# Linear attention plus GELU feed-forward on one core: another order of the input loads ahead of the first matmuls

## Chip, cores and metric

The kernel runs on one core of a Trainium2 chip. The metric is device time in microseconds (us) for one execution; lower is better. Before the change three runs gave a median of 211.41 us (211.33 to 211.56).

## What is computed

One normalised input feeds two branches, and both are added to the input (B = 1, S = 2048 tokens, D = 640, F = 1536, 32 heads of 20 columns; bf16 in and out):

```python
x = A_x
xn = _layernorm(x, axis=-1)
return x + _A_ref(xn, A_wqkv, A_wo) + _B_ref(xn, B_w1, B_b1, B_w2, B_b2)
# _A_ref: q, k, v = xn @ wqkv; phi(t) = where(t > 0, t + 1, exp(t)) + 1e-6
#         o = (phi(q) @ (phi(k)^T v)) / (phi(q) . sum(phi(k)) + 1e-6), per head; o @ wo
# _B_ref: gelu(xn @ w1 + b1) @ w2 + b2
```

## The kernel before

The 2048 tokens are 16 tiles of 128 (t = 0 to 15). `x_in` (named `xPK` in the profile) holds x with the token on the partition, `xn_tm` the normalised x in the same layout, and `xnT` its transpose (feature on the partition), which the matmuls read. The work is written as one list per engine by a small planner class: each instruction goes to the end of its engine's list, in the order of the Python text, and waits for the semaphores of what it reads and overwrites. Nothing is reordered later, so the order of the text is the order on each engine and on SP's DMA queue.

The front, which the change touches, goes as follows.

- **Loads.** SP issues x tile by tile and the weight W1 in four column quarters (`dma_w1`, 480 KB each); x0 is split in two column halves, one from SP and one from ACT. `dma_x(t, n)` loads n tiles from tile t on (160 KB a tile), all through the helper at L242. The order on SP before the loop is: x0's first half, x1, W1 quarters one and two, x2, quarter three, x3, quarter four, x4-5, x6-7. The read of x8-11 is issued behind tile 3's transpose, and that of x12-15 behind tile 8's.
- **Normalise.** For each tile: two statistics instructions on DVE (`ln_half`, L327, one per column half), an aggregate on DVE (`ln_aggr`, L335), a reciprocal root on GpSimd (L341, L343), and a normalise on DVE (`ln_norm`, L355).
- **Transpose.** Tiles 0 to 2 are transposed on PE (`transp2` and `transp`, L313 and L363) into PSUM and copied out: tiles 0 and 1 in two parts, feature blocks 0 to 2 and 3 to 4, one on DVE and one on ACT (`copy2`, L321 and L322), tile 2 by one DVE copy (L371). Tiles 3 to 15 are transposed by DMA (`xnT_dma`, L245), issued on SP, the queue that the x loads use too.
- **First matmuls.** `h_unit(t0, n, jb)` (L382) makes one 128-row block jb of the hidden layer for n tiles: five matmuls, then a GELU on ACT (L386). Block jb needs W1's quarter jb // 3. The order of units is written out by hand:

```python
plan = h_list(0, 1, 0, 3) + ["T1"] + h_list(0, 1, 3, 6) + h_list(1, 1, 0, 6) + h_list(0, 1, 6, 9)
plan += ["T2"] + h_list(1, 1, 6, 9) + h_list(2, 1, 0, JT)
plan += h_list(0, 1, 9, JT) + h_list(1, 1, 9, JT) + h_list(3, 1, 0, JT)
for t, n in ((4, 2), (6, 2), (8, 4), (12, 4)):
    plan += h_list(t, n, 0, JT)
```

At "T1" and "T2" the PE transposes of tiles 1 and 2 are put in, and with them the DVE work of the next tiles. At "T2", after the DVE work of tile 4, `ln_rest()` writes out the normalising and the DMA transposes of all further tiles in one go.

Behind the front, PE computes phi(k), the matrix that joins xn and phi(k), phi(q), the products with Wv and Wo, and at last the output, 17 matmul groups a tile. The change touches no line of these.

Of the kernel before, what the change touches and what calls it, by code (L numbers as in the profile page):

```python
# [6 lines left out]
ACT = mybir.ActivationFunctionType  # L7
P = 128
# [104 lines left out]
def bass_parallel_sum__linear_attn_block__dense_activation_gelu__prompt_kernel(  # L113
# [4 lines left out]
    NT = S // P  # L118
# [3 lines left out]
    DT = D // P  # L122
# [3 lines left out]
    HW = D // 2  # L126
# [3 lines left out]
    Pl = Planner(nc)  # L130
    R_ = Pl.res
# [5 lines left out]
    with contextlib.ExitStack() as es:  # L137
# [3 lines left out]
        x_in = xPK  # L141
# [3 lines left out]
        xnT = xnTf[:].rearrange("p (k s) -> p k s", k=DT)  # L145
# [37 lines left out]
        B_ = [R_("bank%d" % i) for i in range(8)]  # L183
        ring = [0]

        def take(n):
            b = ring[0]
            if n == 2 and b % 2:
                b += 1
            b %= 8  # L190
            ring[0] = (b + n) % 8
            return b

        def bank(b, lo=0, hi=512):
            return ps[:, b * 512 + lo: b * 512 + hi]
# [4 lines left out]
        def halves(ap):  # L200
            return ap.rearrange("p (a n) -> p a n", a=2)

        r_x = [[R_("x%d_%d" % (t, i)) for i in range(2 if t == 0 else 1)] for t in range(NT)]
        r_xr = [R_("xr%d" % c) for c in range(NC)]
        r_xb = [R_("xb%d" % t) for t in range(NT)]
        r_xn = [[R_("xn%d_%d" % (t, i)) for i in range(2 if t == 0 else 1)] for t in range(NT)]
        r_xnT = [[R_("xnT%d_%d" % (t, i)) for i in range(2 if t < 2 else 1)] for t in range(NT)]
# [7 lines left out]
        r_stats = [R_("stats%d" % i) for i in range(4)]  # L215
# [14 lines left out]
        xv = A_x.rearrange("b s d -> (b s) d")  # L230
# [6 lines left out]
        v = "vector"  # L237
        s_ = "scalar"
        pe = "tensor"

        def dma(eng, dst, src, writes, reads=()):
            Pl.ins(eng, lambda e: e.dma_start(dst, src), reads=reads, writes=writes, dma=True)  # L242
# [4 lines left out]
        def dma_x(t, n):  # L247
            dma("sync", x_in[:, t:t + n, :], xv[t * P:(t + n) * P, :].rearrange("(t p) d -> p t d", p=P),
                sum(r_x[t:t + n], []))

        def dma_w1(i):
            lo, hi = W1P[i]
            dma("sync", W1[:, :, lo:hi], w1v[:, :, lo:hi], [r_W1[i]])

        for i, q in enumerate(("sync", s_)):
            dma(q, x_in[:, 0, i * HW:(i + 1) * HW], xv[0:P, i * HW:(i + 1) * HW], [r_x[0][i]])
        dma_x(1, 1)
        dma_w1(0)
        dma_w1(1)
        dma_x(2, 1)  # L260
        dma_w1(2)
        dma_x(3, 1)
        dma_w1(3)
        dma_x(4, 2)
        dma_x(6, 2)

        Pl.ins(v, lambda e: e.memset(warm[:].bitcast(FP32), 0.0), writes=[r_warm])
        Pl.ins(g, lambda e: e.memset(onesm[:], 1.0), writes=[r_ones])
# [5 lines left out]
               reads=[r_ident], writes=[r_ident])  # L274
# [35 lines left out]
        def transp2(t, b0, b1):  # L310
            for lo, hi, b in ((0, 3, b0), (3, DT, b1)):
                pT = bank(b).bitcast(BF16)
                Pl.ins(pe, [(lambda e, k=k, pT=pT, lo=lo: e.transpose(  # L313
                    pT[:, (k - lo) * P:(k - lo + 1) * P], xn_tm[:, t, k * P:(k + 1) * P], ident[:]))
                    for k in range(lo, hi)], reads=[r_xn[t][0 if lo == 0 else -1], r_ident], writes=[B_[b]])

        def copy2(t, b0, b1):
            tok = slice(t * P, (t + 1) * P)
            pA = bank(b0).bitcast(BF16)[:, 0:XA].rearrange("p (k q) -> p k q", q=P)
            pB = bank(b1).bitcast(BF16)[:, 0:D - XA].rearrange("p (k q) -> p k q", q=P)  # L320
            Pl.ins(v, lambda e: e.tensor_copy(xnT[:, 0:3, tok], pA), reads=[B_[b0]], writes=[r_xnT[t][0]])  # L321
            Pl.ins(s_, lambda e: e.activation(xnT[:, 3:DT, tok], pB, ACT.Copy), reads=[B_[b1]],  # L322
                   writes=[r_xnT[t][1]])

        def ln_half(t, h):
            s = t % 4
            Pl.ins(v, lambda e: e.bn_stats(stats[:, s, 6 * h:6 * h + 6], x_in[:, t, h * HW:(h + 1) * HW]),  # L327
                   reads=[r_x[t][min(h, len(r_x[t]) - 1)]], writes=[r_stats[s]])

        def ln_aggr(t):  # L330
            s = t % 4
            if t < 2:
                Pl.ins(v, lambda e: e.tensor_single_scalar(stats[:, s, 2:3], stats[:, s, 2:3], D * EPS, ALU.add),
                       reads=[r_stats[s]], writes=[r_stats[s]])
            Pl.ins(v, lambda e: e.bn_aggr(aggr[:, s, :], stats[:, s, :]),  # L335
                   reads=[r_stats[s]], writes=[r_aggr[s]])
            if t < 2:
                var, r_var = aggr[:, s, 1:2], r_aggr[s]
            else:
                var, r_var = veps[:, s:s + 1], r_veps[s]  # L340
                Pl.ins(g, lambda e: e.tensor_single_scalar(var, aggr[:, s, 1:2], EPS, ALU.add),  # L341
                       reads=[r_aggr[s]], writes=[r_var])
            Pl.ins(g, lambda e: e.tensor_tensor(out=rstd[:, t:t + 1], in0=var, in1=mhalf[:], op=ALU.pow),  # L343
                   reads=[r_var, r_small], writes=[r_rstd[t]])

        def ln_stats(t):
            ln_half(t, 0)
            ln_half(t, 1)
            ln_aggr(t)

        def ln_norm(t):
            s = t % 4
            for i, r in enumerate(r_xn[t]):
                lo, hi = (0, D) if len(r_xn[t]) == 1 else ((0, XA), (XA, D))[i]
                Pl.ins(v, lambda e, lo=lo, hi=hi: e.tensor_scalar(  # L355
                    xn_tm[:, t, lo:hi], x_in[:, t, lo:hi], aggr[:, s, 0:1], rstd[:, t:t + 1],
                    ALU.subtract, ALU.mult),
                    reads=r_x[t] + [r_aggr[s], r_rstd[t]], writes=[r])

        def transp(t):  # L360
            b = take(1)
            pT = bank(b).bitcast(BF16)[:, 0:D]
            Pl.ins(pe, [(lambda e, k=k: e.transpose(pT[:, k * P:(k + 1) * P],  # L363
                                                    xn_tm[:, t, k * P:(k + 1) * P], ident[:]))
                        for k in range(DT)],
                   reads=r_xn[t] + [r_ident], writes=[B_[b]])
            return b

        def xnT_copy(t, b):
            pT = bank(b).bitcast(BF16)[:, 0:D]  # L370
            Pl.ins(v, lambda e: e.tensor_copy(xnT[:, :, t * P:(t + 1) * P],  # L371
                                              pT.rearrange("p (k q) -> p k q", k=DT)),
                   reads=[B_[b]], writes=r_xnT[t])

        def xnT_dma(t):
            dma_t("sync", xnT[:, :, t * P:(t + 1) * P], xn_tm[:, t, :], r_xnT[t], reads=r_xn[t])

        def h_unit(t0, n, jb):
            b = take(1)
            w = n * P  # L380
            tok = slice(t0 * P, t0 * P + w)
            Pl.ins(pe, [(lambda e, k=k: e.matmul(  # L382
                bank(b, 0, w), W1[:, k, jb * P:(jb + 1) * P], xnT[:, k, tok],
                start=(k == 0), stop=(k == DT - 1))) for k in range(DT)],
                reads=[r_W1[FW[jb]]] + sum(r_xnT[t0:t0 + n], []), writes=[B_[b]])
            Pl.ins(s_, lambda e: e.activation(  # L386
                HG[:, jb, tok], bank(b, 0, w), ACT.Gelu_apprx_tanh, bias=b1c[:, jb:jb + 1]),
                reads=[B_[b], r_b1c], writes=[r_HG[t][jb] for t in range(t0, t0 + n)])

        Pl.ins(s_, lambda e: e.activation(b1c[:, 0:1], warm[:, 0:1], ACT.Gelu_apprx_tanh),  # L390
               reads=[r_warm], writes=[r_b1c])
# [24 lines left out]
        def ln_rest():  # L416
            for t in range(4, NT):
                if t + 1 < NT:
                    ln_half(t + 1, 0)
                    ln_half(t + 1, 1)  # L420
                ln_norm(t)
                if t + 1 < NT:
                    ln_aggr(t + 1)
                xnT_dma(t)
                if t == 8:
                    dma_x(12, 4)

        for u in plan:
            if u == "T1":
                b = take(2)  # L430
                transp2(1, b, b + 1)
                copy2(1, b, b + 1)
                ln_stats(2)
                ln_half(3, 0)
                ln_norm(2)
                ln_half(3, 1)
                ln_aggr(3)
            elif u == "T2":
                b = transp(2)
                xnT_copy(2, b)  # L440
                ln_half(4, 0)
                ln_norm(3)
                xnT_dma(3)
                dma_x(8, 4)
                ln_half(4, 1)
                ln_aggr(4)
                ln_rest()
            else:
                h_unit(*u)
# [203 lines left out]
        t = NT - 1  # L653
        xb(t)
        tok = slice(t * P, (t + 1) * P)
        for i, (lo, hi) in enumerate([(0, 320), (320, 512), (512, 640)]):
# [3 lines left out]
            s = t % 2  # L660
            Pl.ins(v, lambda e, lo=lo, hi=hi, b=b: e.tensor_tensor(
                out=out_sb[:, s, lo:hi], in0=bank(b, 0, hi - lo), in1=x_res[:, t, lo:hi], op=ALU.add),
                reads=[B_[b], r_xb[t]], writes=[r_o] + ([r_out[s]] if i == 0 else []))
# [40 lines left out]
```

## Time and profile before

| what | value |
|---|---|
| median of three runs | 211.41 us (211.33 to 211.56) |
| the profiled execution | 211.35 us, of which the profiled span is 209.6 us |
| TensorE (PE) busy | 203.2 us, 97% of the span |
| VectorE (DVE) busy | 108.9 us, 52% |
| ScalarE (ACT) busy | 73.8 us, 35% |
| GpSimd (POOL) busy | 20.0 us, 10% |
| granted TensorE clock | 1.0 |
| hidden-layer matmuls (L382) | 477 records, 52.9 us |
| moved by DMA | 18.16 MB, mean 87 GB/s over the span |

All times in the views are us from the span's start. A row of a timeline gives the start, the time taken, the engine (SPq is SP's list of DMA issues), the line of the kernel, the operation with what it writes and reads, and in square brackets how long the engine stood idle before it and what ended that. For a DMA the row's time is that of the issue; when its data has landed stands in the DMA rows as "us to landing". Busy shares are averages: where a change touches one stage, the waits of that stage count.

### The profile page before, as it was taken

The page shows a single profiled execution, that of the slowest core. Times are in us where ns is not written, and L with a number is a line of the kernel's source. Part 1 is how long each engine was busy: PE and PEld are TensorE (multiplying, and loading weights), DVE is VectorE, ACT ScalarE, POOL GpSimd, SP SyncE. Part 2 cuts the span into 40 slices and gives each one's busy share as a digit, 9 for nine tenths or more (in the row PEclk, how much of TensorE's full clock was granted, in tenths as well). Part 3 has the DMA queues.
Part 4 walks back from the last instruction along what each step waited for, and adds up shares of the span by engine and source line. Part 5 has one row for each costly group of instructions (what it writes and reads, how often), then busy time and mean ns, then how long its engine had stood idle before and what let it go on. Part 6 is the DMA issues. An engine that isn't in the chain of part 4 may idle for free.

```text
span 209.6 us, 3964 instructions
## 1 busy us (share of the span) xinstructions
PE 203.2 (97%) x1616; PEld 140.6 (67%) x1622; DVE 108.9 (52%) x213; ACT 73.8 (35%) x146; POOL 20.0 (10%) x57
## 2 busy tenths in 40 slices
PE   7899699999999999999999999999999999999995
PEld 2799588444447777777757556677777777777775
DVE  4688847000005888999148889633753422523322
ACT  2699588566667445211143556200000000000000
POOL 2134425810011000000000000000000000000000
PEclk9999999999999999999999999999999999999999
DMA  5959965799500000000000000952210110010002
GB/s 147 343 165 190 110 183 111 186 355 341 200 0 0 0 3 0 3 0 0 0 3 0 0 2 14 353 179 57 69 66 31 48 51 31 31 34 31 31 31 66
DMA packets 23515, 18.16 MB, mean 87 GB/s; under 512 B 9928, under 2 KB 23496, under 8 KB 23496
## 3 DMA queue, kind: packets, MB, share of 16 engines
q1 hardware_dynamic: 23136, 17.68, 30.0%
q8 instruction: 13, 0.21, 0.4%
q10 hardware_dynamic: 360, 0.22, 0.4%
q14 instruction: 6, 0.05, 0.1%
HBM read 12.62 MB, written 2.62 MB: 73 GB/s over the span
## 4 chain that ended last, share of the span: by engine, by line
PE 88%; DMA 6%; SPq 2%; DVE 1%; issue 1%; POOL 0%
PE ps L620 35%; PE ps L382 19%; PE ps L494 10%; PE ps L482 10%; PE ps L531 10%; DMA xPK<-in_A_x_dram 3%; DMA xnT<-xn_tm 3%; SPq L242 2%; PE ps L556 1%; PE ps L540 1%; PE ps L571 1%; DVE xn_tm L355 0%; POOL rstd L343 0%; DVE stats L327 0%; PE ps L514 0%
## 5 line engine op out<-in xcount | busy, mean ns | idle before, releaser
L382 PE MATMUL ps<-xnT,W 128*128 128x128 bf16 (+2 forms) x477 | 52.9, 272 | 2.2 <-DMA xnT<-xn_tm 1.9
L620 PE MATMUL ps<-W,HG 128*128 128x320 bf16 (+2 forms) x396 | 54.7, 295 | 0.0
L382 PEld LDWEIGHTS ps<-xnT,W 128*128 128x128 bf16 x480 | 36.8, 98 | 17.9 <-DMA xnT<-xn_tm 2.0
L620 PEld LDWEIGHTS ps<-W,HG 128*128 128x128 bf16 x396 | 38.0, 98 | 14.7 <-issue 0.4
L386 ACT ACTIVATE HG<-ps,b1c 128x128 bf16<-128x128 f32 (+2 forms) x96 | 41.5, 474 | 14.2 <-PE ps L382 12.6
L631 DVE TENSOR_TENSOR W<-ps,xnT 128x640 bf16<-128x640 f32 x15 | 12.4, 824 | 37.1 <-PE ps L620 36.8
L470 ACT ACTIVATE ek<-ps 128x512 bf16<-128x512 f32 (+1 forms) x36 | 23.2, 644 | 20.7 <-PE ps L531 11.0
L471 DVE TENSOR_SCALAR ek<-ek 128x512 bf16<-128x512 bf16 (+1 forms) x36 | 10.9, 303 | 36.8 <-ACT ek L470 35.6
L620 PE MATMUL ps<-Msb,PQ 128*128 128x320 bf16 (+2 forms) x165 | 24.2, 295 | 0.0
L482 PE MATMUL ps<-Wqkv,xnT 128*128 128x320 bf16 x160 | 21.9, 299 | 0.0
L494 PE MATMUL ps<-xPK,xn_tm 128*128 128x320 bf16 x160 | 21.9, 299 | 0.0
L531 PE MATMUL ps<-xnT,Wqkv 128*128 128x512 bf16 x97 | 21.4, 379 | 0.2
L620 PEld LDWEIGHTS ps<-Msb,PQ 128*128 128x128 bf16 x165 | 15.9, 98 | 5.9
L482 PEld LDWEIGHTS ps<-Wqkv,xnT 128*128 128x128 bf16 x160 | 15.6, 98 | 6.3
L494 PEld LDWEIGHTS ps<-xPK,xn_tm 128*128 128x128 bf16 x160 | 15.6, 98 | 6.1
L327 DVE BATCH_NORM_STATS2 stats<-xPK 128x6 f32<-128x320 bf16 x32 | 15.3, 477 | 7.4 <-DMA xPK<-in_A_x_dram 6.7
L531 PEld LDWEIGHTS ps<-xnT,Wqkv 128*128 128x128 bf16 x100 | 11.7, 117 | 9.5
L473 DVE SCALAR_TENSOR_TENSOR PQ<-ps,ek 128x512 bf16<-128x512 f32 x20 | 13.8, 692 | 2.1
L473 DVE SCALAR_TENSOR_TENSOR xPK<-ps,ek 128x640 bf16<-128x640 f32 x16 | 13.2, 825 | 1.7
L506 DVE TENSOR_TENSOR Msb<-Msb,xPK 128x640 f32<-128x640 f32 x14 | 11.6, 826 | 0.5
L498 ACT ACTIVATE W<-ps 128x640 bf16<-128x640 f32 x5 | 3.5, 703 | 18.2 <-PE ps L494 18.2
L355 DVE TENSOR_SCALAR xn_tm<-xPK,aggr,rstd 128x640 bf16<-128x640 bf16 (+2 forms) x17 | 7.2, 431 | 2.5 <-POOL rstd L343 1.5
(57 smaller groups left out, 76.8 us busy)
## 6 DMA issues: line engine op xcount, KB each, us to landing
xnT<-in_A_x_dram SPq DMA_DIRECT2D x4, 640.0 KB, 6.4
Wqkv<-in_A_wqkv_dram SPq DMA_DIRECT2D x3, 800.0 KB, 6.6
out_dram<-W SPq DMA_DIRECT2D x15, 160.0 KB, 1.8
W<-in_B_w_dram SPq DMA_DIRECT2D x4, 480.0 KB, 6.3
W<-in_B_w_dram SPq DMA_DIRECT2D x1, 1920.0 KB, 15.7
xPK<-in_A_x_dram SPq DMA_DIRECT2D x2, 640.0 KB, 4.8
Wo<-in_A_wo_dram SPq DMA_DIRECT2D x1, 800.0 KB, 10.7
xPK<-in_A_x_dram SPq DMA_DIRECT2D x2, 320.0 KB, 7.0
```

What stands on the lines that cost most here:

```text
L327: Pl.ins(v, lambda e: e.bn_stats(stats[:, s, 6 * h:6 * h + 6], x_in[:, t, h * HW:(h + 1) * HW]), reads=[r_x[t][min(h, len(r_x[t]) - 1)]], ...
L382: Pl.ins(pe, [(lambda e, k=k: e.matmul(bank(b, 0, w), W1[:, k, jb * P:(jb + 1) * P], xnT[:, k, tok], start=(k == 0), stop=(k == DT - 1))) ...
L386: Pl.ins(s_, lambda e: e.activation(HG[:, jb, tok], bank(b, 0, w), ACT.Gelu_apprx_tanh, bias=b1c[:, jb:jb + 1]), reads=[B_[b], r_b1c], wri ...
L470: Pl.ins(s_, lambda e: e.activation(e2, src, ACT.Exp), reads=br, writes=[r_ek[s]])
L471: Pl.ins(v, lambda e: e.tensor_scalar(et, et, 1.0, 1e-6, ALU.min, ALU.add), reads=[r_ek[s]], writes=[r_ek[s]])
L473: Pl.ins(v, lambda e: e.scalar_tensor_tensor(out=d2, in0=src, scalar=0.0, in1=e2, op0=ALU.max, op1=ALU.add), reads=br + [r_ek[s]], writes= ...
L482: fns.append(lambda e, k=k, h=h, b=b, t=t: e.matmul(bank(b + h, 0, HW), xnT[:, k, t * P:(t + 1) * P], Wqkv[:, k, D + h * HW:D + (h + 1) * ...
L494: Pl.ins(pe, [(lambda e, t=t, h=h, b=b, f=f, i=i: e.matmul(bank(b + h, 0, HW), xn_tm[:, t, f * P:(f + 1) * P], PK[:, t, h * HW:(h + 1) * H ...
L506: Pl.ins(v, lambda e, t=t: e.tensor_tensor(out=zsum, in0=zsum, in1=PK[:, t, :], op=ALU.add), reads=[r_PK[t], r_zsum], writes=[r_zsum])
L531: Pl.ins(pe, [(lambda e, k=k, j=j, b=b: e.matmul(bank(b), Wqkv[:, k, j:D:DT], xnT[:, k, cc], start=(k == 0), stop=(k == DT - 1))) for k in ...
L620: Pl.ins(pe, [(lambda e, i=i, x=x, bb=bb: e.matmul(bank(bb, 0, x[1] - x[0]), seq[i][0], seq[i][1][:, x[0]:x[1]], start=(i == 0), stop=(i = ...
L631: Pl.ins(v, lambda e: e.tensor_tensor(out=halves(out_sb[:, s, :]), in0=pair(b), in1=halves(x_res[:, t, :]), op=ALU.add), reads=B_[b:b + 2] ...
```

## The change

It puts the loads at the front in another order on SP's queue: x3 in front of W1's third quarter, x4-5 in front of the fourth, x8-11 at the end of the first batch (in front of tile 3's DMA transpose) and x12-15 behind tile 7's transpose instead of tile 8's. x0 is loaded whole by SP. In the copies of tiles 0 and 1 out of PSUM, ACT takes the three-block part and DVE the two-block part. On DVE, tile 3's second statistics move in front of tile 2's normalise, and tile 4's first statistics in front of tile 2's copy.

```diff
-        r_x = [[R_("x%d_%d" % (t, i)) for i in range(2 if t == 0 else 1)] for t in range(NT)]
+        r_x = [[R_("x%d" % t)] for t in range(NT)]
...
-        for i, q in enumerate(("sync", s_)):
-            dma(q, x_in[:, 0, i * HW:(i + 1) * HW], xv[0:P, i * HW:(i + 1) * HW], [r_x[0][i]])
+        dma_x(0, 1)
         dma_x(1, 1)
         dma_w1(0)
         dma_w1(1)
         dma_x(2, 1)
+        dma_x(3, 1)
         dma_w1(2)
-        dma_x(3, 1)
+        dma_x(4, 2)
         dma_w1(3)
-        dma_x(4, 2)
         dma_x(6, 2)
+        dma_x(8, 4)
...
-            Pl.ins(v, lambda e: e.tensor_copy(xnT[:, 0:3, tok], pA), reads=[B_[b0]], writes=[r_xnT[t][0]])
-            Pl.ins(s_, lambda e: e.activation(xnT[:, 3:DT, tok], pB, ACT.Copy), reads=[B_[b1]],
-                   writes=[r_xnT[t][1]])
+            Pl.ins(s_, lambda e: e.activation(xnT[:, 0:3, tok], pA, ACT.Copy), reads=[B_[b0]], writes=[r_xnT[t][0]])
+            Pl.ins(v, lambda e: e.tensor_copy(xnT[:, 3:DT, tok], pB), reads=[B_[b1]], writes=[r_xnT[t][1]])
...
-                   reads=[r_x[t][min(h, len(r_x[t]) - 1)]], writes=[r_stats[s]])
+                   reads=r_x[t], writes=[r_stats[s]])
...
-                if t == 8:
+                if t == 7:
                     dma_x(12, 4)
...
                 copy2(1, b, b + 1)
                 ln_stats(2)
                 ln_half(3, 0)
+                ln_half(3, 1)
                 ln_norm(2)
-                ln_half(3, 1)
                 ln_aggr(3)
+                ln_half(4, 0)
             elif u == "T2":
                 b = transp(2)
                 xnT_copy(2, b)
-                ln_half(4, 0)
                 ln_norm(3)
                 xnT_dma(3)
-                dma_x(8, 4)
                 ln_half(4, 1)
                 ln_aggr(4)
                 ln_rest()
```

## The prediction

> **What bounds the kernel now.** I read the page first (busy shares and slices), then the chain of waits, then the timelines of PE, SP and DVE over the first 25 us, then the DMA rows of narrow windows. The page says TensorE:
>
> ```profile
> PE 203.2 (97%) x1616; PEld 140.6 (67%) x1622; DVE 108.9 (52%) x213; ACT 73.8 (35%) x146; POOL 20.0 (10%) x57
> PE   7899699999999999999999999999999999999995
> PEclk9999999999999999999999999999999999999999
> ```
>
> PE is full in every slice but the first six, at full clock. So the change, which touches only the front, can win only what PE idles there. The PE timeline has one large hole:
>
> ```profile
> 6.95 1.00 PE L382 MATMUL ps<-xnT,W 128*128 128x128 bf16 x15
> ...
> 11.52 0.44 PE L363 MATMUL ps<-ident,xn_tm 128*128 128x128 bf16 x5
> 11.80 9.38 PE L382 MATMUL ps<-xnT,W 128*128 128x128 bf16 x165
> 23.04 39.16 PE L382 MATMUL ps<-xnT,W 128*128 128x256 bf16 x237 [1.86 <-DMA xnT<-xn_tm]
> ```
>
> The 165 matmuls from 11.80 start 0.0558 us apart, so the next could have started at 11.80 + 9.21 = 21.01; it started at 23.04. The hole is 2.03 us (1.86 by modelled ends). Behind 23.04 PE runs without a hole of note, so a shift there passes to the end one for one. The chain names what the hole waits for:
>
> ```profile
> 15.85 6.48 DMA xnT<-xn_tm
> 22.33 0.70 issue
> 23.04 13.26 PE ps L382 x120
> ```
>
> The first 256-token unit needs tiles 4 and 5. Tile 4's DMA transpose, issued at 15.85, lands at 22.33; the "issue" after it is really tile 5's, issued 17.41, which took 5.5 and landed at 22.94. SP's timeline shows what stood in front of them:
>
> ```profile
> 13.76 1.31 SPq L245 DMA_TRANSPOSE xnT<-xn_tm  x1
> 15.12 0.57 SPq L242 DMA_DIRECT2D xPK<-in_A_x_dram  x1
> 15.85 8.03 SPq L245 DMA_TRANSPOSE xnT<-xn_tm  x5
> ```
>
> Tile 3's transpose, with an empty queue, took 2.67 us to land (16.43). Then comes the 640 KB read of x8-11 (lands 19.67), and the next two transposes take 6.5 and 5.5. The DMA rows of 19 to 21 us add a second cause:
>
> ```profile
> GB/s 333 297 287 302 277 282 287 246 210 169 256 251 272 584 256 425 236 266 251 251 266 154 154 97 41 15 10 0 0 0 0 0 0 0 5 10 5 10 5 10
> q14 instruction: 1, 0.01, 5.8%
> q8 instruction: 1, 0.02, 3.3%
> ```
>
> Two instruction fetches start at 19.68 and 19.76 (1.07 and 1.85 us in the trace). From 20.4 the queue trickles at 5 to 10 GB/s: [...] the rest hold their packets open (1.3 us instead of 0.018). Last, DVE:
>
> ```profile
> 10.54 0.49 DVE L327 BATCH_NORM_STATS2 stats<-xPK 128x6 f32<-128x320 bf16 x1 [0.68 <-DMA xPK<-in_A_x_dram]
> ...
> 12.89 0.49 DVE L327 BATCH_NORM_STATS2 stats<-xPK 128x6 f32<-128x320 bf16 x1 [0.40 <-DMA xPK<-in_A_x_dram]
> ```
>
> It waits for x3 (lands 10.52) and x4-5 (12.87), both queued behind W1 quarters; that is why tile 3's normalise runs only at 13.30.
>
> **The change part by part.**
>
> *Landings.* In steady flow (340 GB/s from 5 to 12 us) each transfer lands a fixed step after the one in front: a single x tile 0.47, a W1 quarter 1.48, an x pair 0.80 to 0.86. Before: x2 8.57, W1 quarter three 10.05, x3 10.52, quarter four 12.01, x4-5 12.87, x6-7 13.67. Reordered: x2 8.57, x3 9.04, quarter three 10.52, x4-5 11.38, quarter four 12.87, x6-7 13.67, x8-11 13.67 + 2 x 0.80 = 15.27. Bytes and DMA count on SP stay the same.
>
> *x0 whole.* ACT loses one issue (0.41 us, ACT idle then: nothing). DVE's first statistics started at 3.06 on the first half; the second half landed at 3.22 and its statistics started at 3.66. The row nearest to a whole 160 KB tile is x1: 3.18 us, so x0 at 3.98; statistics at 4.00 and 4.53, 0.87 late. The Trainium skill, "DMA: Bandwidth & Descriptors", section "Anatomy of one DMA", fits 2.0 us plus bytes at 436 GB/s: 2.38 us for a tile, so 3.18, and statistics at 3.20 and 3.73, 0.07 late. The same fit gives 2.19 for a half, where the trace has 2.24 and 2.41; x1 is late by a single packet of 0.96 us. I lean to the rule: +0.1, ends 0 and 0.87. Nothing covers it: statistics, reciprocal root, normalise, transposes and copies follow in a row into the matmul at 6.95 (W1's first quarter lands at 6.63 and hides 0.3 at most of a gain).
>
> *Copy halves swapped.* The three-block half goes to ACT: 0.383 for 256 columns and 0.75 ns per column more, an estimate from the 0.37 of its 128-column rows and the 0.703 of 640, gives 0.48; DVE's two-block copy takes 0.29 by its 0.36 and 0.49 rows. For tile 0, ACT starts 0.11 earlier, because the three-block bank is ready first: 6.31 + 0.48 = 6.79 against 6.81. Nothing. For tile 1 it ends 0.1 later (8.75) with 0.25 us to spare before tile 1's first unit at about 9.0.
>
> *Tile 2 and W1 quarter three.* Both statistics of x3 now fit ahead of tile 2's normalise (9.8 to 10.8; reciprocal root ready at 10.83): normalise at 10.86 instead of 10.96. Nothing won, since PE reaches those transposes only at 11.52. Quarter three is first used three units of 0.279 before them, at 10.68, and lands at 10.52: slack 0.63 shrinks to 0.16, or 0.26 with x0's shift. Cost 0 to 0.4.
>
> *Tile 4's first statistics ahead of tile 2's copy.* This is an added wait: DVE holds at x4-5 with tile 2's copy, hence PE's first tile-2 unit (12.64), behind it. Tile 3's aggregate ends at 11.45, x4-5 lands at 11.38, statistics 11.47 to 11.96, copy at 12.00 as now. Tie. Each tenth that x4-5 lands after 11.5 costs a tenth. I book 0.1, ends 0 and 0.6.
>
> *Tile 3.* Reciprocal root ready at 12.4, normalise behind the copy at 12.55 to 13.0 (13.30 before), transpose issued at 13.0 instead of 13.76, but now behind x8-11 on the one queue. Two rows show a transpose behind a 640 KB read: tile 9's landed 0.58 after it, tile 4's 2.66 after it, in the fetches. So 15.85 to 17.93 here; another fetch falls at 12.34, so I take 17.0. PE needs it at 17.66 plus the shift. Cost 0, ends 0 and 0.3.
>
> *Tiles 4 and 5.* The DVE cadence is 1.56 us per tile. Transposes at 15.1 and 16.65 (15.85 and 17.41 before); with no read in front each takes its lone 2.67: 17.8 and 19.3, ahead of the fetch at 19.68 and of the need at 21.2. The hole closes: -2.03. x12-15 goes out behind tile 7's transpose at about 21; tiles 8 to 11 then land by 30, needed at about 34. Hidden.
>
> Sum: -2.03 + 0.1 + 0.1 = -1.83 us. The profiled execution took 211.35 (span 209.6 and 1.75 around it), 0.06 below the median: 209.5 from it, 209.6 from the median 211.41.
>
> **The rivals.**
>
> *x0 late as x1 was* (chance 0.10). For it: x1's own row. Against: both halves were in by 3.22. Cost 0.87 instead of 0.1: 210.35.
>
> *A new wait in the front* (0.10): quarter three, x4-5 in front of tile 2's copy, or tile 3's transpose at its late end. For it: slacks of 0.16, 0.1 and 0.7. Against: each is late by tenths. 0.5 to 1.2 lost: 210.1 to 210.9.
>
> *x8-11 held back on SP, tile 3 behind it* (0.18). The place is the wait of tile 3's first unit at 17.66. SP's issues already stall when much is outstanding: x3's took 1.44 us and the next pairs 1.06 and 0.92, against 0.43 to 0.53. If x8-11 cannot be issued until about 12.9, it lands 4.5 later (its own row) at 17.4, and the transpose 2.66 behind at 20.1: a stall of 2.4 in place of the 2.03, and with x0's 0.1 a time of 211.9. It decides at a landing of 19.6 (no change); past 20.0 it is slower. Against: x6-7's issue ended at 7.78, so at that pace x8-11 is out by 10.
>
> *The change doesn't do what it says*: that the hole is the fetches' alone and stays. Then tile 5 must still be in flight at 19.68; my 19.3 leaves 0.4 us. If hit, it lands at 21.3 to 22.0 and 0.2 to 0.9 of the hole stays: inside the range.
>
> **How the numbers follow.** 0.2% is 0.42 us, about what this kernel's measurement tells from no change. The clean case (0.62) gives 209.1 to 210.1, likeliest 209.6. With the first two rivals, 0.82 lies at 209.1 to 210.9: faster 0.82, and that is the range. The held read (0.18) splits into 0.05 within 0.42 us of 211.41 and 0.13 slower.
>
> **What would show it.** Right: no hole at the start of the 256-token units, which begin near 21.2; x3's statistics without a wait; x4-5 at about 11.4; tile 3's transpose landed by 17.7; tiles 4 and 5 in 2.7 us each. Wrong: the first statistics after 3.5, a hole at 10.7, 12.6 or 17.7, an x8-11 issue later than 11, or the hole merely moved to tile 3.

## The result and the profile after

The changed kernel takes 209.42 us (median of four runs, 209.23 to 209.78) against 211.45 before in the same measurement: ratio 0.9906, 95% interval 0.9889 to 0.9923. That is 2.03 us less; the forecast was 209.6 with faster as the likeliest outcome. The page after, busy shares and slices:

```profile
PE 203.4 (98%) x1622; PEld 140.7 (68%) x1622; DVE 108.8 (52%) x213; ACT 73.9 (36%) x146; POOL 20.1 (10%) x57
PE   7899999999999999999999999999999999999995
```

PE's work is the same (203.4 us for 203.2); only the span is shorter (207.6 for 209.6), and the 6 in the fifth slice has become a 9. PE's timeline has the hidden-layer rows in one piece:

```profile
6.79 1.00 PE L381 MATMUL ps<-xnT,W 128*128 128x128 bf16 x15
...
7.91 3.51 PE L381 MATMUL ps<-xnT,W 128*128 128x128 bf16 x60
11.26 0.44 PE L362 MATMUL ps<-ident,xn_tm 128*128 128x128 bf16 x5
11.54 48.62 PE L381 MATMUL ps<-xnT,W 128*128 128x128 bf16 x405
```

The chain of waits dates the start of the 256-token units, 23.04 before and 21.00 now:

```profile
11.70 9.21 PE ps L381 x165
20.91 0.08 issue
21.00 39.16 PE ps L381 x240
```

The difference is 2.04 us, and nothing behind it is given back: the output matmuls begin at 131.27 in this chain and at 133.31 in the one before. The 2.04 comes in two parts. The first hidden-layer matmul starts at 6.79 instead of 6.95 and the stop of 0.09 us in front of the fourth unit (it had waited for W1's second quarter, landed at 8.11, now 7.83) is gone: 0.26 together. The hole has shrunk from 2.03 to 0.25 us: 1.78. What is left of it is told by SP and the DMA rows. SP:

```profile
5.97 2.26 SPq L242 DMA_DIRECT2D xPK<-in_A_x_dram  x2
...
12.70 8.32 SPq L245 DMA_TRANSPOSE xnT<-xn_tm  x5
21.07 0.58 SPq L242 DMA_DIRECT2D xPK<-in_A_x_dram  x1
```

The read of x8-11 left at 7.54 (the second of the first row) and landed at 15.72. Tile 3's transpose, issued at 12.70, landed at 16.38, 0.66 behind that read and a good 1 us ahead of 17.4, where PE needed it. The DMA rows at the issues of tiles 4 and 5 (14.79 and 16.35), then those of 18 to 19 us:

```profile
xnT<-xn_tm SPq DMA_TRANSPOSE x1, 2.6
...
xnT<-xn_tm SPq DMA_TRANSPOSE x1, 4.6
```

```profile
GB/s 236 215 164 195 195 236 236 215 195 226 164 779 83 62 51 31 10 11 0 0 0 0 0 0 0 0 0 0 0 0 0 0 0 0 0 0 328 0 0 0
...
q14 instruction: 1, 0.01, 7.3%
q8 instruction: 1, 0.02, 5.9%
```

Tile 4 took 2.6 us, as long as a lone one, although the read and tile 3 were still in flight at its issue. Tile 5 took 4.6: its data flows at some 200 GB/s until 18.28, where an instruction fetch begins (the spike of 779), and thins out to nothing by 18.45. It landed at 20.91; PE had run dry at 20.75. DVE, last, waits for x3 and x4-5 no more:

```profile
9.51 0.97 DVE L326 BATCH_NORM_STATS2 stats<-xPK 128x6 f32<-128x320 bf16 x2
10.60 0.45 DVE L354 TENSOR_SCALAR xn_tm<-xPK,aggr,rstd 128x640 bf16<-128x640 bf16 x1
10.96 0.20 DVE L334 BATCH_NORM_AGGREGATE aggr<-stats 128x2 f32<-128x12 f32 x1
11.16 0.49 DVE L326 BATCH_NORM_STATS2 stats<-xPK 128x6 f32<-128x320 bf16 x1
11.74 0.49 DVE L370 COPY xnT<-ps 128x640 bf16<-128x640 bf16 x1
```

x3 (landed 8.76) is ready when its statistics come up at 9.51; tile 4's first statistics start at 11.16, just behind x4-5's landing at 11.13, and end at 11.65, before the copy of tile 2 starts at 11.74. The added wait is empty, with 0.03 us to spare at x4-5's landing.

### The profile page after: what moved, and what is told of

Its sections match the earlier page's. It is cut to its first block, busy times and chain, and to the rows that moved or that the text cites. A ratio compares the mean times of both kernels' runs of the same rounds, so it can differ in the third digit from the quotient of the medians.

```text
span 207.6 us, 3967 instructions
## 1 busy us (share of the span) xinstructions
PE 203.4 (98%) x1622; PEld 140.7 (68%) x1622; DVE 108.8 (52%) x213; ACT 73.9 (36%) x146; POOL 20.1 (10%) x57
## 4 chain that ended last, share of the span: by engine, by line
PE 96%; DVE 1%; DMA 1%; issue 0%
PE ps L618 36%; PE ps L381 25%; PE ps L492 10%; PE ps L480 10%; PE ps L529 10%; PE ps L554 1%; DMA xPK<-in_A_x_dram 1%; DVE stats L326 1%; PE ps L538 1%; PE ps L569 1%; PE ps L313 0%; PE ps L512 0%; PE ps L298 0%; DVE W L659 0%; DVE xn_tm L354 0%
## 5 line engine op out<-in xcount | busy, mean ns | idle before, releaser
L529 PE MATMUL ps<-xnT,Wqkv 128*128 128x512 bf16 x100 | 21.9, 379 | 0.0
```

The source lines that it names most:

```text
L529: Pl.ins(pe, [(lambda e, k=k, j=j, b=b: e.matmul(bank(b), Wqkv[:, k, j:D:DT], xnT[:, k, cc], start=(k == 0), stop=(k == DT - 1))) for k in ...
```

## The experiments

**The read of x8-11 behind tile 3's transpose again.**

```diff
         dma_x(6, 2)
-        dma_x(8, 4)
...
                 xnT_dma(3)
+                dma_x(8, 4)
```

> The changed kernel with one part undone: the read of x8-11 is issued behind tile 3's transpose again; all else stays. My theory (the read between tile 3's transpose and those of tiles 4 and 5 makes the hole): x8-11 issued at about 14.0 lands at 18.5, tile 5's transpose 0.6 to 3.3 us behind it, at 19.6 to 22.4 instead of 20.9; the hole in front of the 256-token units is then up to 1.7 us wide, the time 209.4 to 211.0, likeliest 210.4. Rival A (the DVE chain that runs 1.06 us earlier is what helped): tile 5 lands 1.06 us earlier than before the change whatever the read does, at 21.9, the hole is 1.1 us, the time 210.3. Rival B (the hole is the instruction fetches' alone): no change from 209.4.

Measured: 210.44 us, ratio to before 0.997 (0.9941 to 0.9998). Its profile has a hole of 1.08 us (20.82 to 21.90), with tiles 4 and 5 taking 5.9 and 5.4 us to land:

```profile
12.74 1.32 SPq L245 DMA_TRANSPOSE xnT<-xn_tm  x1
14.11 0.57 SPq L242 DMA_DIRECT2D xPK<-in_A_x_dram  x1
14.83 6.46 SPq L245 DMA_TRANSPOSE xnT<-xn_tm  x4
```

```profile
11.60 9.38 PE L380 MATMUL ps<-xnT,W 128*128 128x128 bf16 x165
21.90 18.44 PE L380 MATMUL ps<-xnT,W 128*128 128x256 bf16 x144 [0.92 <-issue]
```

Nine of its twelve executions took 210.2 to 210.6 us, three 212.2 to 212.3. By the medians this one place in the queue is worth about 1 us on top of the other parts, and the fetches alone are not the hole: rival B falls. My theory and rival A had expected nearly the same number here, so between them the run decides nothing. The next one does.

**x8-11 alone, on the kernel before.**

```diff
         dma_x(6, 2)
+        dma_x(8, 4)
...
                 xnT_dma(3)
-                dma_x(8, 4)
```

> The kernel before with one part done alone: x8-11 issued at the end of the first batch, in front of tile 3's transpose; W1 order, x0, copies and DVE order as before. My theory: tiles 4 and 5, issued at 15.85 and 17.41 as before, land at about 18.5 and 20.1, or 21.0 to 21.5 where an instruction fetch hits tile 5; the hole of 2.0 us shrinks to 0 to 0.5 us and the time falls to 209.5 to 210.0. Rival A (the earlier DVE chain did it): tile 5 still lands at about 22 or later, the time stays above 210.8. Rival B (fetches alone): 211.4 as before.

Measured: 209.96 us against 211.31, ratio 0.9935 (0.9913 to 0.9958). PE's timeline:

```profile
11.67 9.38 PE L383 MATMUL ps<-xnT,W 128*128 128x128 bf16 x165
21.50 39.16 PE L383 MATMUL ps<-xnT,W 128*128 128x256 bf16 x240 [0.45 <-issue]
```

The 256-token units start at 21.50. PE had run dry at 20.88, so 0.62 us of hole is left. Tile 4, issued at 15.79, took 2.6 us; tile 5, issued at 17.35 and met by the fetch at 18.27, took 4.1 and landed at 21.41. The DVE chain of tile 5 ended where it did before the change (issue at 17.35 for 17.41), so rival A falls too: moving the read is by itself worth some 1.4 us. The other parts move the chain forward by about another us (tile 5's issue 16.35 for 17.35), of which 0.5 is still to be had. The parts overlap: 1.4 alone and 0.9 by the others without it make more than the 2.03 of all, because the hole cannot shrink below nothing.

**W1's quarters in front of x3 and x4-5 again, DVE's order kept.**

```diff
         dma_x(2, 1)
-        dma_x(3, 1)
         dma_w1(2)
-        dma_x(4, 2)
+        dma_x(3, 1)
         dma_w1(3)
+        dma_x(4, 2)
         dma_x(6, 2)
```

> The changed kernel with W1's quarters three and four in front of x3 and x4-5 again, but DVE's new order kept (tile 4's first statistics ahead of tile 2's copy). My theory: the order of loads and DVE's order belong together; x4-5 lands at about 12.6, DVE holds tile 2's copy until 13.1, PE waits 1.3 us for its first tile-2 unit, and everything behind moves with it: 210.7 (210.3 to 211.1). Rival: the wait is hidden or made up in the hole later on, 209.4 to 209.7.

Measured: 210.65 us, the expected time, ratio to before 0.9963 (0.9943 to 0.9982). The wait that the forecast had priced at 0 to 0.6 is now there. DVE:

```profile
10.17 1.02 DVE L326 BATCH_NORM_STATS2 stats<-xPK 128x6 f32<-128x320 bf16 x2 [0.57 <-DMA xPK<-in_A_x_dram]
...
12.57 0.49 DVE L326 BATCH_NORM_STATS2 stats<-xPK 128x6 f32<-128x320 bf16 x1 [0.92 <-DMA xPK<-in_A_x_dram]
12.98 0.47 DVE L370 COPY xnT<-ps 128x640 bf16<-128x640 bf16 x1
```

and PE:

```profile
11.60 0.45 PE L362 MATMUL ps<-ident,xn_tm 128*128 128x128 bf16 x5
11.89 1.00 PE L381 MATMUL ps<-xnT,W 128*128 128x128 bf16 x15
13.52 8.55 PE L381 MATMUL ps<-xnT,W 128*128 128x128 bf16 x150 [0.63 <-DVE xnT L370]
```

x4-5 lands at 12.55, tile 2's copy goes out at 12.98 instead of 11.74, and PE stands in front of tile 2 (three units from 11.89 are done at 12.73 by starts, the next begins at 13.52: 0.79). A smaller stop of 0.32 in front of tile 2's PE transposes comes from x3; together that is 1.1 of the 1.3 expected. With the old order of loads DVE's new order costs: the kernel that has neither and moves x8-11 alone took 209.96.

**DVE's order back, loads as changed.**

```diff
                 ln_half(3, 0)
-                ln_half(3, 1)
                 ln_norm(2)
+                ln_half(3, 1)
                 ln_aggr(3)
-                ln_half(4, 0)
...
                 xnT_copy(2, b)
+                ln_half(4, 0)
                 ln_norm(3)
```

> The changed kernel with DVE's order as before (tile 3's second statistics behind tile 2's normalise, tile 4's first statistics behind tile 2's copy); loads stay as changed. My theory: nothing for PE. Tile 2's copy does not wait in either, tile 3's normalise and its transpose go out 0.4 to 0.5 later (13.1 to 13.2 instead of 12.7) but land behind x8-11 anyway, at 16.4 to 16.8, ahead of the 17.4 where PE needs it; tile 4's chain ends where it did: 209.4. Rival: tiles 4 and 5 move by the same 0.4 and the hole grows to 0.6: 209.8.

Measured: 209.8 us (209.42 to 210.48), ratio to before 0.9917 (0.9885 to 0.9948). I had expected nothing; the number is the rival's, though its interval does not exclude 209.4. SP's view shows two things that I had missed:

```profile
13.64 2.26 SPq L245 DMA_TRANSPOSE xnT<-xn_tm  x1
...
17.29 1.24 SPq L245 DMA_TRANSPOSE xnT<-xn_tm  x1
```

```profile
21.73 18.44 PE L381 MATMUL ps<-xnT,W 128*128 128x256 bf16 x144 [0.48 <-issue]
```

Tile 3's transpose leaves at 13.64 instead of 12.70, and its issue takes 2.26 us instead of 1.32, which holds SP until 15.90 and tile 4's behind it by 0.2. Tile 5's leaves at 17.29, as soon as DVE has normalised it, takes 4.3 us across the fetch at 18.33, and PE starts the 256-token units at 21.73 with 0.65 us of hole. Some 0.35 of the 0.94 is this execution's later x2 (8.65 for 8.30); the rest is the order, because tile 3's normalise now waits for its reciprocal root and tile 4's aggregate comes 0.94 later (14.05 for 13.11).

**x0 in halves again.**

```diff
-        r_x = [[R_("x%d" % t)] for t in range(NT)]
+        r_x = [[R_("x%d_%d" % (t, i)) for i in range(2 if t == 0 else 1)] for t in range(NT)]
...
-        dma_x(0, 1)
+        for i, q in enumerate(("sync", s_)):
+            dma(q, x_in[:, 0, i * HW:(i + 1) * HW], xv[0:P, i * HW:(i + 1) * HW], [r_x[0][i]])
...
-                   reads=r_x[t], writes=[r_stats[s]])
+                   reads=[r_x[t][min(h, len(r_x[t]) - 1)]], writes=[r_stats[s]])
```

> The changed kernel with x0 in two halves again, one from SP and one from ACT. The forecast booked +0.1 us for the whole tile; the profile after shows instead that the statistics began at 3.10 without a wait between the halves and that W1's first quarter landed 0.30 us earlier (6.33 for 6.63). If x0 whole is what brought the weights forward, the first hidden-layer matmul goes back by 0.1 to 0.15 and the stop of 0.1 us in front of the fourth unit returns (second quarter at 8.11): 209.6. Rival: the earlier weights come from the run and not from x0; 209.4, first matmul at about 6.8.

Measured: 209.49 us (208.94 to 209.75), between the two expectations and not told from x0 whole. In its profile the halves landed at 2.86 and 3.05 and the first hidden-layer matmul came at 6.66, earlier than with x0 whole, but W1's second quarter landed at 8.26 and PE stopped for it:

```profile
8.30 3.52 PE L382 MATMUL ps<-xnT,W 128*128 128x128 bf16 x60 [0.37 <-DMA W<-in_B_w_dram]
```

So the 0.16 us at the first matmul are no work of x0. For the other 0.1, the stop for W1's second quarter, that stays open: over the eleven profiles with x0 whole the quarter landed at 7.47 to 8.19, with halves at 7.97 to 8.26 in three. The ranges overlap, as the rival says, but all three with halves lie in the late part.

**The copy halves swapped back.**

```diff
-            Pl.ins(s_, lambda e: e.activation(xnT[:, 0:3, tok], pA, ACT.Copy), reads=[B_[b0]], writes=[r_xnT[t][0]])
-            Pl.ins(v, lambda e: e.tensor_copy(xnT[:, 3:DT, tok], pB), reads=[B_[b1]], writes=[r_xnT[t][1]])
+            Pl.ins(v, lambda e: e.tensor_copy(xnT[:, 0:3, tok], pA), reads=[B_[b0]], writes=[r_xnT[t][0]])
+            Pl.ins(s_, lambda e: e.activation(xnT[:, 3:DT, tok], pB, ACT.Copy), reads=[B_[b1]], writes=[r_xnT[t][1]])
```

> The changed kernel with the copy halves as before: DVE takes the three-block part, ACT the two-block part. In the forecast the swap was worth nothing. By the profile after, both copies of tile 0 end at 6.65; swapped back, DVE's ends at about 6.55 and ACT's, 0.38 long behind the last transpose at 6.32, at 6.74: the first hidden-layer matmul 0.1 later, 209.5. Rival: nothing at all, since PE's own queue (the last filler matmul ends at 6.75 by the profile) holds the first matmul as long: 209.4.

Measured: 209.39 us. The first hidden-layer matmul came at 6.92 instead of 6.79, as expected, but the time shows nothing of it: inconclusive at this size. The profiles do tell the two apart. Where tile 0's five PE transposes start 0.32 us from first to last, the first hidden-layer matmul starts 1.02 behind the first of them in the seven profiles with the swap, and 1.11 in the two without it (this one and x8-11 alone).

**x12-15 behind tile 8's transpose again.**

```diff
-                if t == 7:
+                if t == 8:
                     dma_x(12, 4)
```

> The changed kernel with the read of x12-15 behind tile 8's transpose again. The forecast called this part hidden: tiles 8 to 11 land by 30 and are needed at 34, so nothing, 209.4. Rival: the transposes of tiles 6 and 7 or the statistics of tile 12 feel it and the time moves by 0.2 or more.

Measured: 209.3 us. Hidden, as forecast. In its profile tile 5 landed at 20.43 and there was no hole.

**The fetch moved, first try.** If the instruction fetch comes at a count of PE's instructions, more of them in PE's idle time, ahead of the first statistics, bring it forward. The second argument of `filler` is the columns of a matmul (P is 128).

```diff
-        def filler(n):
+        def filler(n, w=512):
...
-        filler(9)
+        filler(1)
+        filler(72, P)
```

> The changed kernel with PE's nine idle-time matmuls of 512 columns replaced by one of 512 and 72 of 128 columns (about the same time, 64 matmuls and weight loads more), so that PE's instruction fetches fall about 3.6 us earlier in the 128-token stage. Theory F (the 0.25 us left of the hole is tile 5's transpose, held 1.9 us by the fetch that starts at 18.28): the fetch moves to about 14.7, tile 5 lands at 19.0 to 19.6, the hole closes and the time falls by 0.25 to 209.2. Rival: tile 5 is held by the other transposes or by the fetch on the other queue at 18.92; it lands at about 20.9 again and the time stays 209.4.

Measured: 211.01 us where 209.2 was expected. Most of the 128-column matmuls took 0.107 us each, not 0.056, and the row of them ran from 1.25 to 8.5; everything behind started 2.5 us later. The profile still says something. Tile 5's transpose, issued at 19.04, fell between two of PE's fetches (17.62 and 24.13) and took 2.6 us, the first tile 5 to do so. That there was no hole proves nothing here, since PE came 2.5 us later.

**The fetch moved, second try.**

```diff
...
-        filler(9)
+        filler(36, P)
```

> The changed kernel with PE's nine idle-time matmuls of 512 columns replaced by 36 of 128 columns, which at the 0.10 us apiece seen in the first try at this fit into the same idle time. PE's instruction count ahead of the 128-token stage grows by 27 matmuls and loads, so the fetch that started at 18.28 falls at about 16.8. Theory F (tile 5's transpose is held by that fetch): the fetch hits tile 4's transpose instead (landing about 18.5 to 19.3, needed at 20.8), tile 5 lands at 19.5 to 20.2, the hole closes, 209.2. Rival (tile 5 is held by something else): tile 5 lands at 20.9 and 0.25 us of hole stays, 209.4.

Measured: 209.18 us (208.88 to 209.3), ratio 0.9898 (0.9879 to 0.9916). The fetch fell at 16.90 (the spike of 697 below), on tile 4, which took 4.2 us instead of 2.6 and landed at 19.03. Tile 5, queued behind it, landed at 20.34: 4.0 us, a little later than expected but ahead of PE, and the hole was gone. The rows are those of 16.5 to 17.5, of the issues of tiles 4 and 5, and PE's:

```profile
GB/s 236 215 184 205 205 195 174 236 225 225 175 135 123 83 92 697 0 0 0 0 0 0 0 0 0 0 0 0 0 0 0 0 0 0 0 0 0 0 0 0
q8 instruction: 1, 0.02, 5.8%
...
xnT<-xn_tm SPq DMA_TRANSPOSE x1, 4.2
...
xnT<-xn_tm SPq DMA_TRANSPOSE x1, 4.0
...
11.58 28.73 PE L381 MATMUL ps<-xnT,W 128*128 128x128 bf16 x313
```

Counted from PE's first tile-2 unit the fetch came at 5.32 us instead of 6.74, so 1.42 earlier; 27 matmuls at 0.0558 are 1.51. The delay moved with the fetch:

| kernel | PE's fetch starts | tile 4: issued, us to landing | tile 5: issued, us to landing |
|---|---|---|---|
| changed | 18.28 | 14.79, 2.6 | 16.35, 4.6 |
| x8-11 alone | 18.27 | 15.79, 2.6 | 17.35, 4.1 |
| fetch moved, first try | 17.62 | 17.28, 2.8 | 19.04, 2.6 |
| fetch moved, second try | 16.90 | 14.81, 4.2 | 16.38, 4.0 (behind tile 4) |

In the first try the fetch also lies inside a transpose, tile 4's, but it starts only 0.34 us behind the issue, and the data of that transpose moved from 18.4 on; it cost 0.2. In the rows with the long times the fetch starts 0.9 to 2.1 us behind the issue.

**Tile 4 first.**

```diff
-        for t, n in ((4, 2), (6, 2), (8, 4), (12, 4)):
+        plan += h_list(4, 1, 0, 2) + h_list(5, 1, 0, 2) + h_list(4, 2, 2, JT)
+        for t, n in ((6, 2), (8, 4), (12, 4)):
```

> The changed kernel with the first two hidden-layer blocks of tiles 4 and 5 made one tile at a time, tile 4 first (its transpose landed at 17.4), so that PE has 0.56 us of work before it needs tile 5 (landed at 20.91, hole from 20.75). If the rest of the hole is only the wait for tile 5: the hole closes at a price of 4 x 0.279 - 2 x 0.543 = 0.03 us, 209.2. Rival: PE's start of this stage is bound by something else as well, 209.4.

Measured: 209.07 us (208.93 to 209.35), ratio 0.9897 (0.9878 to 0.9915). Tile 5 landed at 21.21 in its profile, and PE went through without a hole. Whether it beats the changed kernel needed both on one chip:

> The changed kernel once more, on the chip on which the next kernel runs, so that the two can be compared directly. 209.4 by the first measurement; a hole of 0 to 0.3 us in front of the 256-token units, by where tile 5's transpose lands (20.4 to 21.2 in the profiles so far).

> The kernel with the first two blocks of tiles 4 and 5 one tile at a time, beside the changed kernel on the same chip. If the rest of the hole was worth its 0.25 us in most executions: 0.1 to 0.3 below the changed kernel. Rival: tile 5's landing differs from execution to execution so much that most have no hole, and the two are alike within 0.1.

Measured: the changed kernel 209.1, ratio 0.9893 (0.9866 to 0.992); tile 4 first 209.09, ratio 0.989 (0.986 to 0.9921). Alike: the rival holds. The changed kernel's chain here goes from tile 2 to the end of the hidden layer in one piece:

```profile
11.70 48.21 PE ps L381 x405
```

Tile 5 landed at 20.57, so the 0.25 us of the first profile is not a standing loss (the run with the copies swapped back had 0.29 again). No version of these is shown to be faster than the changed kernel.

## Why the prediction was right

**The hole and its size.** The step held: PE idles only in the front, the hole of 2.03 us is the wait for tile 5's transpose, and what closes it passes to the end one for one. The read of x8-11 alone brought 1.4 us. The term was 2.03 and measured 1.78 in the first profile, because tile 5 was booked at its lone 2.67 us and took 4.6. The failing number is the place of the fetch: I set it at 19.68 as before, 0.4 us behind tile 5's landing; it started at 18.28. Counted from PE's first tile-2 unit, the fetch starts at 6.5 to 7.0 us in the ten profiles with the same count of instructions up to there and no stop in between, and at 7.9 in the one before the change. There it starts as the read of x8-11 lands (19.68 for 19.67), so the read seems to have held the fetch as well; no run tests that. The case in which the fetch hits tile 5 had been named, with 0.2 to 0.9 of the hole left; 0.25 is in it.

**Landings.** x3 8.76 (forecast 9.04), quarter three 10.23 (10.52), x4-5 11.13 (11.38), quarter four 12.63 (12.87), x6-7 13.55 (13.67), x8-11 15.72 (15.27). The steps up to quarter four held within 0.05, and the row stands 0.3 earlier, which lies within the spread (x2 landed at 7.9 to 8.7 over the profiles). The last two steps did not hold: x6-7 took 0.92 instead of 0.80, and x8-11 2.17 instead of 1.60 (1.6 to 3.0 over the profiles). Tile 3 had the room for it.

**x0 whole.** The rule came closer: x0 landed in 2.28 us (rule 2.38, row of x1 3.18; x1 itself took 3.05, and 2.2 to 3.2 in other profiles). The Trainium skill, "DMA: Bandwidth & Descriptors", section "Anatomy of one DMA — SWDGE (gpsimd) path", states this fit for DMAs of the gpsimd path, and x0 goes over SP's queue, so the 2.38 was an estimate from a figure for another path; x0 whole took 2.1 to 2.3 in every profile here. The term of +0.1 was nothing: the second statistics started at 3.63 instead of 3.66, since with one load they follow without the 0.11 us that lay between them. The halves run does not tell it from nothing.

**Copies.** Forecast at nothing; this term was missed by 0.1 at the first matmul. ACT's three-block copy was to start at 6.31 and end at 6.79, about as late as the copy before; it started at 6.16 and took 0.49, and the first matmul starts 0.09 us sooner behind the transposes than without the swap. That is most of the 0.16 at the first matmul. The times are too coarse to show it.

**Tile 4's statistics ahead of the copy.** Booked at 0.1, it cost 0, because x4-5 landed 0.25 earlier than forecast, by 0.03 us before its statistics came up, so with some luck. The mechanism is real: with x4-5 at 12.55 the wait took 0.79 us of PE.

**Tile 3.** Forecast to land at 17.0 of a range from 15.85 to 17.93, it landed at 16.38, 0.66 behind the read, near the favourable row.

**x12-15.** Hidden, as forecast.

**The slow rival** did not come. x8-11 left SP at 7.54, not near 12.9. But its mechanism, SP held up while much is outstanding, showed itself in the run with DVE's order back (2.26 us for one issue, which held tile 4's transpose by 0.2) and in x8-11 alone (1.92, which held nothing: tile 4's left when DVE had it ready).

The main term was right in its mechanism and near in size. That the sum is as near, -1.83 forecast and -2.03 measured, is in part luck: the 0.25 of hole left over is cancelled by 0.26 in the front that nobody had booked, and the two terms of +0.1 proved to be nothing.

**Left open.** How much of the hole before was the read and how much the fetches was not separated: tile 4 and tile 5 had both. With the read out of the way and the fetch on tile 5, some 0.6 us of hole stays (x8-11 alone). A transpose behind a 640 KB read without a fetch near landed 0.62 behind it (tile 8 after the change: 26.89 behind 26.27). By this row tile 4 would have landed at 20.3 before, and tile 5, by the 0.56 between tiles 8 and 9, at about 20.9, just in time for 21.0; this is an estimate, and no run shows it. It would mean that the hole before took both, the read and a fetch behind it.

## What to carry to other kernels

Where the bound engine has one hole, follow the last transfer it waits for back to its queue and ask what stands in front of it. Here a bulk read that is needed late, put ahead of the first DMA transpose instead of between those that PE waits for, brought 1.4 us by itself; behind the last of them it was not tried. An instruction order that is built on early loads must move together with the loads: DVE's new order with the old loads took 210.65 us, neither of the two (x8-11 alone) 209.96, both together 209.42. Of a tight landing, give the range over executions and not one profile's value: the 0.25 us that was left in one profile was absent in the next.

## What the runs showed that I had not expected

- Where a 16 KB instruction fetch (about 1.0 us) starts 0.9 to 2.2 us behind the issue of a DMA transpose, the transpose takes 4.0 to 4.7 us instead of 2.6 (tile 4 or 5 in all eleven profiles where this happened with no bulk read in front), and the delay follows the fetch from tile 5 to tile 4. The fetch is no fixed clock: between the changed kernel's two profiles it started at 18.28 and 18.52, and before the change at 19.68.
- 128-column matmuls at the start of the kernel come 0.107 us apart, in the main stage 0.056; in the first try with the moved fetch the distance changes at 7.2 us, in the middle of their row. The granted clock of 1.0 does not speak against a slower clock at the start: in the seven traces with clock records the first record begins 3.9 to 6.6 us into the span (6.1 before the change), and ahead of it the profile shows 1.0 for want of a record. The Trainium skill, "TensorE: Matmul & The Clock Gate", in Part 1, has 106.7 ns for them while the array is cold and 55.6 warm, which agrees.
- An issue of a DMA transpose on SP takes 1.2 to 1.3 us in most places, but 1.4 to 2.3 in some with reads and transposes outstanding; the longest held the next transpose by 0.2.
